# Batch 0 loads halved over two queues, filler matmuls on zeros, a revised start order, and one v cast moved to GpSimd, in a fused attention and channel-mix kernel

## The chip, the cores and the metric

The kernel runs on one core of one Trainium2 chip. The metric is the device time of one execution in microseconds; lower is better. The record marks each run as fast or slow (a program can fall into a slower state whatever its kernel). The kernel before took 221.51 us (median of 3 runs, 221.03 to 221.57). A profiled execution has a span a little shorter than its device time (219.7 us for a run of 221.48 us).

## The reference, cut to what matters

```python
# q, k, v: (batch 8, heads 8, seq 576, head_dim 64)
q_s = softmax(q, over head_dim)             # per row
k_s = softmax(k, over seq)                  # per column
kv  = einsum('bhsd,bhse->bhde', k_s, v)     # 64 x 64 per head
x   = einsum('bhsd,bhde->bhse', q_s, kv)    # -> (8, 576, 512)
x_prev = x shifted by one row
xk = mu_k * x + (1 - mu_k) * x_prev
xr = mu_r * x + (1 - mu_r) * x_prev
k  = relu(xk @ w_k)                         # 512 -> 1024
v  = (k * k) @ w_v                          # 1024 -> 512
out = sigmoid(xr @ w_r) * v
```

## The kernel before: the parts that matter

Two groups ("group 0" and "group 1") of four heads make up a batch. Each group goes through an attention pass: exp of q and of k and a cast of v (ScalarE), a softmax sum and scaling of q (VectorE), kv and transposes and x (TensorE), copies out of PSUM (ScalarE), then difference and mix into xk and xr (VectorE). The second half, the "units" of 512, 384 or 256 columns, multiplies xk by w_k (tile kfp), takes a relu on ScalarE (rel), squares on VectorE (k2), multiplies by w_r (rp) and w_v (vp).

The start is written out by hand; everything after it is ordered by a scheduler when the program is built.

```python
def emit_load(b, g, queues=None):
    t = ldpool.tile([128, 3, 2, J * D], F32, tag="raw", name="raw")
    for i, src in enumerate((q, k, v)):
        ...                                  # 576 KB each
        queue = queues[i] if queues else nc.gpsimd
        ld.append(queue.dma_start(out=t[:, i, :, :], in_=ap))

first = emit_load(0, 0, (nc.sync, nc.scalar, nc.sync))
...                                          # mu
emit_load(0, 1, (nc.scalar, nc.sync, nc.scalar))
...
emit_weights(first[2])                       # w_k, w_r, w_v on the GpSimd queue, after batch 0's first v
emit_load(1, 0)                              # batch 1, same queue, behind the weights
emit_load(1, 1)
with tc.manual_schedule(engines={PE, DVE, Activation}):   # shortened
    emit_mu()
    a0 = Attention(0, 0); a1 = Attention(0, 1)
    a0.exp(0); a0.exp(1); a0.norm_q(); a0.cast_v(nc.scalar.copy)
    a1.exp(0)
    a0.kv("mm"); a0.transpose_q(); a0.copy_qt(); a0.weights()
    a1.exp(1); a1.norm_q()
    a0.x(0); a0.x(1)
    a1.cast_v(nc.scalar.copy)
    a1.kv("mm"); a1.transpose_q(); a1.copy_qt()
    a0.diff(); a0.mix(0)
    a1.weights()
    a1.x(0); a1.x(1); a1.diff(); a1.mix(0)
    a0.mix(1); a1.mix(1)
...                                          # then units, with attention of later batches between their pieces
for pair in range(B // 2):
    for c0, n in UNITS:
        advance(...)
        for c in unit(pair, c0, n, 4 if pair == 0 and c0 == 0 else 1):
            cols += c
            advance(...)                     # so many attention steps of later batches
```

The softmax here doesn't subtract the row's maximum and nothing guards it: scores larger than these inputs give would overflow.

Of the kernel before, what the change touches and what calls it, by code (L numbers as in the profile page):

```python
# [13 lines left out]
BF16 = mybir.dt.bfloat16  # L14
# [4 lines left out]
def kernel(  # L19
# [18 lines left out]
    nc = tc.nc  # L38

    B, H, S, D = q.shape  # L40
# [3 lines left out]
    J = S // 64  # L44
# [5 lines left out]
    const = ctx.enter_context(tc.tile_pool(name="const", bufs=1))  # L50
# [10 lines left out]
    SYNC = mybir.DependencyInfo(mybir.DependencyClass.Sync, mybir.DependencyReason.DATA)  # L61
    ctx.enter_context(tc.manual_schedule(engines={mybir.EngineType.Pool}))

    def emit_load(b: int, g: int, queues=None):
        t = ldpool.tile([128, 3, 2, J * D], F32, tag="raw", name="raw")
        ld = []
        for i, src in enumerate((q, k, v)):
            ap = bass.AP(tensor=src.tensor,
                         offset=src.offset + (b * H + 2 * g) * S * D,
                         ap=[[J * D, 128], [4 * S * D, 2], [1, J * D]])  # L70
            queue = queues[i] if queues else nc.gpsimd
            ld.append(queue.dma_start(out=t[:, i, :, :], in_=ap))  # L72
        raw[b, g] = t
        return ld

    first = emit_load(0, 0, (nc.sync, nc.scalar, nc.sync))
    mu_sb = const.tile([8, 128], F32, name="mu_sb")
    for m, src in enumerate((moe_mu_k, moe_mu_r)):
        ap = bass.AP(tensor=src.tensor, offset=src.offset, ap=[[64, 4], [256, 2], [1, 64]])
        nc.sync.dma_start(out=mu_sb[4 * m:4 * m + 4, :].rearrange("p (u e) -> p u e", u=2),  # L80
                          in_=ap)
    emit_load(0, 1, (nc.scalar, nc.sync, nc.scalar))
    warm = const.tile([1, 1], F32, name="warm")
    nc.vector.memset(warm[:], 0.0)
    nc.scalar.activation(out=warm[:], in_=warm[:], func=ACT.Exp)


    ident = const.tile([128, 128], BF16, name="ident")
    make_identity(nc, ident[:])
    identf = const.tile([8, 8], F32, name="identf")  # L90
# [18 lines left out]
    def emit_weights(gate):  # L109
        def part(dst, src, n, u, c0, c1):  # L110
            ap = bass.AP(tensor=src.tensor, offset=src.offset + 4 * u * D * n + c0,
                         ap=[[n, 64], [D * n, CT], [1, c1 - c0]])
            return nc.gpsimd.dma_start(out=dst[64 * u:64 * u + 64, :, c0:c1], in_=ap)

        for h in range(2):
            for u in range(2):
                ld = part(wk_bf, moe_w_k, F, u, 512 * h, 512 * h + 512)
                if gate is not None:
                    tc.add_manual_dep(ld.ins, gate.ins.name, SYNC)
                gate = None  # L120
        for u in range(2):
            part(wr_bf, moe_w_r, C, u, 0, C)
        n = FT // 2
        for h in range(2):
            ap = bass.AP(tensor=moe_w_v.tensor,
                         offset=moe_w_v.offset + h * n * 128 * C,
                         ap=[[C, 128], [128 * C, n], [1, C]])
            nc.gpsimd.dma_start(out=wv_bf[:, h * n:(h + 1) * n, :], in_=ap)
# [3 lines left out]
    def emit_mu():  # L132
        mup = psum.tile([128, 8], F32, tag="mm", bufs=4, name="mup")
        nc.tensor.transpose(out=mup[:], in_=mu_sb[:], identity=identf[:])  # L134
        nc.vector.tensor_copy(out=mu[:], in_=mup[:])
# [2 lines left out]
    xpair = {}  # L138
    box = [0]

    class Attention:
        def __init__(self, b: int, g: int):
            self.b, self.g = b, g
            self.t = raw.pop((b, g))
            self.vv = vvs[box[0] % 3]
            self.xb = xbs[box[0] % 3]
            box[0] += 1
            if b // 2 not in xpair:
                xpair[b // 2] = (xpool.tile([128, CT, 2 * S], BF16, tag="xk", name="xk"),
                                 xpool.tile([128, CT, 2 * S], BF16, tag="xr", name="xr"))  # L150
            self.eqk = apool.tile([128, 2, J, 2, D], BF16, tag="eqk", name="eqk")
# [19 lines left out]
                out=self.qs[:].rearrange("p j (u d) -> p (j u) d", u=2), in0=eq,  # L171
                in1=rrec[:, :, None].to_broadcast((128, 2 * J, D)), op=ALU.mult)

        def kv(self, tag: str):
            if tag == "att":
                t = psum.tile([128, 2, 512], F32, tag="att", bufs=2, name="kvp")
                self.kvp = [t[:, 0, :], t[:, 1, :]]
            else:
                self.kvp = [psum.tile([128, 512], F32, tag="mm", bufs=4, name="kvp")[:, :]
                            for _ in range(2)]  # L180
            for j in range(J):
                for hf in range(2):
                    r = slice(64 * hf, 64 * hf + 64)
                    nc.tensor.matmul(  # L184
                        self.kvp[hf][:, 0:129],
                        lhsT=self.eqk[r, 1, j, :, :].rearrange("p u d -> p (u d)"),
                        rhs=self.vv[r, j, 0:129], start=(j == 0), stop=(j == J - 1))
# [18 lines left out]
            self.qt = apool.tile([128, J, 128], BF16, tag="qt", name="qt")  # L206
            nc.scalar.copy(out=self.qt[:], in_=self.qtp[:, 0:J, :])  # L207

        def x(self, hf: int):
            self.xp = psum.tile([128, 1024], F32, tag="att", bufs=2, name="xp")  # L210
            for c, e in ((0, 8), (8, J)):
                nc.tensor.matmul(self.xp[:, 64 * c:64 * e], lhsT=self.w[:, hf, :],  # L212
                                 rhs=self.qt[:, c:e, 64 * hf:64 * hf + 64],
                                 start=True, stop=True)
            nc.scalar.copy(out=self.xb[:, hf, 64:64 + S], in_=self.xp[:, 0:S])  # L215
# [90 lines left out]
            pass  # L306


    emit_weights(first[2])
    emit_load(1, 0)  # L310
    emit_load(1, 1)
    with tc.manual_schedule(engines={mybir.EngineType.PE, mybir.EngineType.DVE,
                                     mybir.EngineType.Activation}):
        emit_mu()
        a0 = Attention(0, 0)
        a1 = Attention(0, 1)
        a0.exp(0)
        a0.exp(1)
        a0.norm_q()
        a0.cast_v(nc.scalar.copy)  # L320
        a1.exp(0)
        a0.kv("mm")
        a0.transpose_q()
        a0.copy_qt()
        a0.weights()
        a1.exp(1)
        a1.norm_q()
        a0.x(0)
        a0.x(1)
        a1.cast_v(nc.scalar.copy)  # L330
        a1.kv("mm")
        a1.transpose_q()
        a1.copy_qt()
        a0.diff()
        a0.mix(0)
        a1.weights()
        a1.x(0)
        a1.x(1)
        a1.diff()
        a1.mix(0)  # L340
        a0.mix(1)
        a1.mix(1)
# [57 lines left out]
```

## Time and profile before

| kernel before | |
|---|---|
| device time | 221.51 us |
| TensorE busy, 60 to 200 us | 138.25 of 140 us |
| first exp of batch 1 (q, group 0) | 28.95 us, after a 3.68 us wait for its data |
| xk of group 1 ready | 27.8 us |
| first relu | 30.02 us |

First the activity rows of the profile page. Each digit is the busy share, in tenths, of one fortieth of the span (5.5 us here); PEclk is the TensorE clock that was granted, in tenths of full speed.

```profile
PE   0156599988999999999999999999999999999991
...
ACT  2645279999977779676929696949736392644340
...
PEclk9999969999999999999999999999999999999999
DMA  6999999999999791897085220232131400340414
```

TensorE has little to do in the first four or five slices and is full from then on. The DMA engines are full from 5 us on, for a dozen slices.

The same in stretches: start and end in us and length, then busy time of TensorE, of weight loads, of VectorE, ScalarE and GpSimd, the granted clock, the DMA share and the GB/s moved.

```profile
20.00:30.00 10.00, 7.08 (x27) 3.08 (x26) 5.46 (x15) 3.35 (x4) 4.26 (x6) 0.88 1.16 288
30.00:40.00 10.00, 9.78 (x67) 4.62 (x66) 9.36 (x20) 10.00 (x17) 3.74 (x6) 0.95 1.04 391
40.00:60.00 20.00, 18.34 (x141) 9.58 (x140) 19.93 (x45) 20.00 (x29) 8.31 (x12) 1.00 1.03 400
60.00:80.00 20.00, 19.92 (x140) 10.71 (x139) 19.79 (x46) 15.16 (x26) 4.95 (x7) 1.00 0.94 348
80.00:200.00 120.00, 118.33 (x810) 61.82 (x809) 96.54 (x223) 83.33 (x136) 6.35 (x9) 1.00 0.35 105
```

From 60 us on TensorE idles 1 to 2% of the time.

ScalarE's timeline around 24 us: start, duration, engine, line, operation, output and input, count, and in brackets the idle time before it and what ended that.

```profile
24.09 1.18 ACT L215 CAST xb_109<-xp 128x576 bf16<-128x576 f32 x2 [1.92 <-PE xp L212]
28.95 1.16 ACT L154 ACTIVATE eqk<-raw 128x1152 bf16<-128x1152 f32 x1 [3.68 <-DMA raw<-in_q_dram]
30.02 1.07 ACT L276 ACTIVATE rel<-kfp 128x512 bf16<-128x512 f32 x2
30.97 1.16 ACT L154 ACTIVATE eqk<-raw 128x1152 bf16<-128x1152 f32 x1
32.03 1.08 ACT L276 ACTIVATE rel<-kfp 128x512 bf16<-128x512 f32 x2
```

The first line is group 1's x, copied out of PSUM. Then ScalarE waits 3.68 us for batch 1's q, and from there exps and relus alternate.

TensorE's timeline, the same columns:

```profile
20.80 2.77 PE L270 MATMUL kfp<-xk,wk_bf 128*128 128x512 bf16 x6
23.36 1.10 PE L212 MATMUL xp<-qt,w 128*128 128x512 bf16 x4
24.30 0.59 PE L270 MATMUL kfp<-xk,wk_bf 128*128 128x512 bf16 x2
27.82 6.73 PE L270 MATMUL kfp<-xk,wk_bf 128*128 128x512 bf16 x23 [2.92 <-DVE xk L232]
...
35.84 1.03 PE L284 MATMUL rp<-wr_bf,xr 128*128 128x512 bf16 x4
```

Six kfp matmuls take 2.77 us, about 0.43 us from one to the next; in the second half of the 23 they come every 0.216 us. In the slow part the granted clock is 0.50 (28 to 31 us). (From 20 to 24 us the profile gives a clock of 1.00, although the matmuls there are just as slow. So early in a span the spacing of the matmuls is the safer sign, and the first digits of PEclk are not to be relied on.) The wait of 2.92 us is for group 1's xk.

VectorE makes that xk first and takes batch 1's softmax sum (rsum) afterwards:

```profile
27.01 0.76 DVE L232 TENSOR_TENSOR xk<-xm,xb_109 128x1152 bf16<-128x1152 bf16 x1
...
31.64 1.35 DVE L166 TENSOR_REDUCE rsum<-eqk 128x18 f32<-128x1152 bf16 x1
```

### The profile page before, as it was taken

What the parts mean: (1) busy time and instruction counts of PE and PEld (TensorE: products, weight loads), DVE (VectorE), ACT (ScalarE), POOL (GpSimd) and SP (SyncE); (2) the same over time, 40 slices, a digit from 0 to 9 for tenths busy, and PEclk for the clock granted to TensorE, in tenths of its full rate; (3) what the DMA queues carried; (4) which work ended last, traced back from release to release, by engine and by line L of the source; (5) the groups of instructions that cost most, each with busy time, mean ns of one, the idle gap of its engine ahead of it and who ended that gap; (6) DMA issues with size and microseconds to landing.
All of it is one profiled execution on the core that took longest, in us unless ns stands there. A gap on an engine that the chain in (4) does not pass through costs nothing.

```text
span 219.7 us, 3641 instructions
## 1 busy us (share of the span) xinstructions
PE 193.5 (88%) x1313; PEld 101.6 (46%) x1313; DVE 166.3 (76%) x384; ACT 147.7 (67%) x230; POOL 35.8 (16%) x56
## 2 busy tenths in 40 slices
PE   0156599988999999999999999999999999999991
PEld 0134134534547454445557443546465444554650
DVE  1196389999999998889798998888787758483431
ACT  2645279999977779676929696949736392644340
POOL 1294252433431210230030000000000000000000
PEclk9999969999999999999999999999999999999999
DMA  6999999999999791897085220232131400340414
GB/s 215 397 158 199 262 402 388 393 400 403 404 393 406 273 343 71 256 298 288 3 264 201 49 51 0 57 90 48 36 88 24 95 3 22 73 95 5 108 36 95
DMA packets 16171, 40.62 MB, mean 185 GB/s; under 512 B 2072, under 2 KB 4632, under 8 KB 16152
## 3 DMA queue, kind: packets, MB, share of 16 engines
q0 software_dynamic: 8736, 27.40, 38.0%
q1 hardware_dynamic: 6600, 11.22, 18.0%
q10 hardware_dynamic: 816, 1.77, 2.2%
q8 instruction: 10, 0.16, 0.3%
q14 instruction: 9, 0.07, 0.1%
HBM read 33.56 MB, written 9.44 MB: 196 GB/s over the span
## 4 chain that ended last, share of the span: by engine, by line
PE 60%; ACT 19%; DVE 13%; DMA 3%; issue 2%; SPq 1%; DVEq 0%; ACTq 0%
PE vp L291 22%; PE kfp L270 19%; PE rp L284 11%; ACT eqk L154 5%; ACT qt L207 4%; ACT rel L276 4%; DMA mu_sb<-in_moe_mu_r_dram 3%; PE kvp L184 3%; PE qtp L202 3%; PE xp L212 2%; DVE rsum L166 2%; DVE xk L232 2%; DVE qs L170 2%; ACT xb_105 L215 2%; ACT xb_109 L215 1%
## 5 line engine op out<-in xcount | busy, mean ns | idle before, releaser
L270 PE MATMUL kfp<-xk,wk_bf 128*128 128x384 bf16 (+2 forms) x384 | 72.6, 335 | 4.3 <-DVE xk L232 3.7
L276 ACT ACTIVATE rel<-kfp 128x512 bf16<-128x512 f32 (+2 forms) x96 | 45.4, 518 | 20.5 <-PE kfp L270 19.5
L270 PEld LDWEIGHTS <-wk_bf 128*128 128x128 bf16 x384 | 36.3, 99 | 30.3 <-issue 8.5
L154 ACT ACTIVATE eqk<-raw 128x1152 bf16<-128x1152 f32 x32 | 37.5, 1204 | 9.7 <-DMA raw<-in_q_dram 5.9
L294 DVE SCALAR_TENSOR_TENSOR ot<-th,vp 128x512 f32<-128x512 f32 x36 | 24.6, 683 | 17.3 <-PE vp L291 12.5
L287 ACT ACTIVATE th<-rp 128x512 f32<-128x512 f32 x36 | 22.7, 631 | 21.7 <-PE rp L284 20.7
L284 PE MATMUL rp<-wr_bf,xr 128*128 128x512 bf16 x144 | 37.0, 379 | 0.0
L207 ACT COPY qt<-qtp 128x1152 bf16<-128x1152 bf16 x16 | 18.2, 1136 | 7.7 <-PE qtp L202 7.5
L166 DVE TENSOR_REDUCE rsum<-eqk 128x18 f32<-128x1152 bf16 x16 | 21.6, 1348 | 1.6 <-ACT eqk L154 1.5
L170 DVE TENSOR_TENSOR qs<-eqk,rrec 128x1152 bf16<-128x1152 bf16 x16 | 21.7, 1355 | 0.8
L230 DVE TENSOR_SCALAR xm<-xd,mu 128x576 bf16<-128x576 bf16 x64 | 21.6, 378 | 0.4
L284 PEld LDWEIGHTS <-xr 128*128 128x128 bf16 x144 | 13.3, 98 | 13.8
L72 POOL DMA_DIRECT2D raw<-in_q_dram x14 | 10.0, 713 | 52.9 <-ACT vv_111 L160 24.0
L212 PE MATMUL xp<-qt,w 128*128 128x512 bf16 x64 | 13.5, 302 | 2.6 <-ACT qt L207 2.3
L184 PEld LDWEIGHTS <-eqk 64*128 64x128 bf16 x288 | 9.4, 100 | 9.2 <-issue 8.3
L202 PE MATMUL qtp<-ident,qs 128*128 128x128 bf16 x144 | 11.6, 231 | 1.5 <-DVE qs L170 1.5
L202 PEld LDWEIGHTS <-qs 128*128 128x128 bf16 x144 | 9.8, 103 | 4.1 <-DVE qs L170 1.8
L212 PEld LDWEIGHTS <-w 128*128 128x128 bf16 x64 | 6.3, 103 | 11.0 <-issue 6.1
L72 POOL DMA_DIRECT2D raw<-in_v_dram x14 | 10.0, 711 | 8.4 <-DMA raw<-in_q_dram 5.8
L72 POOL DMA_DIRECT2D raw<-in_k_dram x14 | 10.0, 711 | 5.7 <-DMA raw<-in_v_dram 3.0
L195 DVE SCALAR_TENSOR_TENSOR w<-kvp,rz,mask 128x128 bf16<-128x128 f32 x32 | 9.7, 345 | 0.0
L134 PE MATMUL mup<-identf,mu_sb 8*128 8x8 f32 x1 | 0.2, 243 | 9.8 <-DMA mu_sb<-in_moe_mu_r_dram 9.8
(83 smaller groups left out, 238.7 us busy)
## 6 DMA issues: line engine op xcount, KB each, us to landing
out_dram<-ot SPq DMA_DIRECT2D x72, 128.0 KB, 2.4
raw<-in_q_dram POOLq DMA_DIRECT2D x14, 576.0 KB, 12.4
raw<-in_k_dram POOLq DMA_DIRECT2D x14, 576.0 KB, 12.7
raw<-in_v_dram POOLq DMA_DIRECT2D x14, 576.0 KB, 13.1
wk_bf<-in_moe_w_k_dram POOLq DMA_DIRECT2D x4, 256.0 KB, 6.5
wv_bf<-in_moe_w_v_dram POOLq DMA_DIRECT2D x2, 512.0 KB, 12.4
raw<-in_k_dram ACTq DMA_DIRECT2D x1, 576.0 KB, 5.6
raw<-in_q_dram SPq DMA_DIRECT2D x1, 576.0 KB, 5.2
```

The source lines that it names most:

```text
L72: ld.append(queue.dma_start(out=t[:, i, :, :], in_=ap))
L154: nc.scalar.activation(out=self.eqk[:, i, :, :, :], in_=self.t[:, i, :, :].rearrange("p u (j d) -> p j u d", d=D), func=ACT.Exp)
L166: nc.vector.reduce_sum(out=rsum[:], in_=eq, axis=AX.X)
L170: nc.vector.tensor_tensor(out=self.qs[:].rearrange("p j (u d) -> p (j u) d", u=2), in0=eq, in1=rrec[:, :, None].to_broadcast((128, 2 * J, ...
L202: nc.tensor.transpose(out=self.qtp[:, j, :], in_=self.qs[:, j, :], identity=ident[:])
L207: nc.scalar.copy(out=self.qt[:], in_=self.qtp[:, 0:J, :])
L212: nc.tensor.matmul(self.xp[:, 64 * c:64 * e], lhsT=self.w[:, hf, :], rhs=self.qt[:, c:e, 64 * hf:64 * hf + 64], start=True, stop=True)
L270: nc.tensor.matmul(kfp[:, 0:n], lhsT=wk_bf[:, ct, fc * 128:(fc + 1) * 128], rhs=xk[:, ct, c0:c0 + n], start=(ct == 0), stop=(ct == CT - 1))
L276: nc.scalar.activation(out=rel[:, 0:n], in_=kfp[:, 0:n], func=ACT.Relu, scale=HALF_ROOT)
L284: nc.tensor.matmul(rp[:], lhsT=xr[:, ct, c0 + 128 * m:c0 + 128 * m + 128], rhs=wr_bf[:, ct, :], start=(ct == 0), stop=(ct == CT - 1))
L291: nc.tensor.matmul(vp[:], lhsT=k2[:, ft, 128 * m:128 * m + 128], rhs=wv_bf[:, ft, :], start=(ft == 0), stop=(ft == FT - 1))
L294: nc.vector.scalar_tensor_tensor(out=ot[:], in0=th[:], scalar=1.0, in1=vp[:], op0=ALU.add, op1=ALU.mult)
```

## The change

Its intent is to shorten the start. The two head blocks of each batch 0 load go as separate halves over the SyncE and the ScalarE queue, in the order in which they are needed. Matmuls on a tile of zeros fill TensorE's idle time, so that the slow clock is left earlier. mu moves off the front of TensorE and VectorE. Group 1's v cast goes to GpSimd, which takes 1.2 us off ScalarE; batch 1's loads, issued by GpSimd too, come after that cast.

```diff
-            queue = queues[i] if queues else nc.gpsimd
-            ld.append(queue.dma_start(out=t[:, i, :, :], in_=ap))
+            if b > 0:
+                ld.append(nc.gpsimd.dma_start(...))
+            else:
+                for u, queue in ((0, nc.sync), (1, nc.scalar)):
+                    ld.append(queue.dma_start(out=t[:, i, u, :], ...))
...
+    zeros = const.tile([128, 512], BF16, name="zeros")
+    nc.vector.memset(zeros[:], 0.0)
...
+    def filler(dst, count: int):
+        for _ in range(count):
+            nc.tensor.matmul(dst, lhsT=zeros[:, 0:128], rhs=zeros[:], start=True, stop=True)
...
-    emit_weights(first[2])
-    emit_load(1, 0)
-    emit_load(1, 1)
+    emit_weights(first[5])
     with tc.manual_schedule(...):
-        emit_mu()
         a0 = Attention(0, 0)
         a1 = Attention(0, 1)
         a0.exp(0)
+        a0.norm_q()
         a0.exp(1)
-        a0.norm_q()
         a0.cast_v(nc.scalar.copy)
+        a0.kv("mm", 20)              # 20 filler matmuls first
+        a0.transpose_q()
+        a0.weights()
         a1.exp(0)
-        a0.kv("mm")
-        a0.transpose_q()
         a0.copy_qt()
-        a0.weights()
+        a1.cast_v(nc.gpsimd.tensor_copy)
+        emit_load(1, 0)
+        emit_load(1, 1)
         a1.exp(1)
         a1.norm_q()
-        a0.x(0)
+        a0.x(0, 5)
         a0.x(1)
-        a1.cast_v(nc.scalar.copy)
-        a1.kv("mm")
+        emit_mu()
+        a1.kv("mm", 4)
         a1.transpose_q()
         a1.copy_qt()
+        a1.weights()
         a0.diff()
         a0.mix(0)
-        a1.weights()
-        a1.x(0)
+        a1.x(0, 4)
         a1.x(1)
```

## The prediction

> **What bounds the kernel now.** Three stretches, from the windows and the timeline. (a) 0 to 27.8 us: TensorE mostly waits, at last 2.9 us for VectorE's xk of group 1, ready at 27.8 (waits view). (b) 36 to 58 us: the chain of waits is nearly all ScalarE (20.0 of 20 us busy in 40:60; TensorE 18.3). (c) After 58 us TensorE is busy 97 to 100%. DMA is full from 5 to 70 us, 393 GB/s on raw inputs. Batch 1's first q, queued behind 5.2 MB of weights, lands only at 28.9 us; ScalarE waits 3.7 us for it.
>
> **What the change offers.** Smaller first pieces, mu off the front of TensorE and VectorE, one cast (1.17 us) off ScalarE, filler against the slow clock. In the trace 512-column matmuls come every 0.427 us until about 31 us (granted clock 0.50 at 28 to 31) and every 0.216 us after; the first long row has about 8 slow ones, 1.8 us. The Trainium skill, "TensorE: Matmul & The Clock Gate", Part 1, says that a busy window releases the clock and an idle one (3.4 us) takes it away; the trace agrees with the first half. As meant, xk of group 1 could be ready near 22 us: minus 5 or 6 us.
>
> **What the built order does.**
> 1. ScalarE's queue holds six load issues, the last two waiting for earlier loads to land (semaphore reuse), all ahead of the activation table load (1.28 us). First exp: about 8 us instead of 5.97. Hidden by 2.
> 2. ScalarE now has exp of batch 1's q BEFORE the two copies of group 1's x, and exp k, the v cast and both exps of batch 1's group 1 BEFORE the first relu. Before, the x copies ran at 24.1 us and relus were interleaved. VectorE has batch 1's sum and scaling ahead of group 1's mix; TensorE has kv of batch 1 ahead of the second half of kfp. All wait for batch 1's data. Splitting loads doesn't bring those earlier: bytes are the same, DMA was already full ("DMA: Bandwidth & Descriptors", Issuing engines are not separate DMA queues: all interleave on the same 16 engines; the trace shows no more than about 400 GB/s with three queues).
>
> **Sum from trace durations.** q lands 28.9; exp to 30.0; x copies to 31.1; VectorE sum, shift, reciprocal, diff, scale, mix, add (1.35+0.2+0.27+0.77+1.36+0.65+0.77) to about 35.5: xk of group 1 comes 7.7 us later than 27.8. TensorE idles from about 21 to 33 and is slow again. The first unit's kfp, with batch 1's kv, transposes, x and first rp, ends near 44.2 instead of 37.5 (+6.7 on TensorE); ScalarE in the same state near 44.8 against 40.6 (+4.2). TensorE's idle time between 36 and 58 (about 1.8 us) absorbs some: net about +5.
>
> **Prediction: 226.3 us**, range 223.0 to 230.0. Chances: faster 0.07, same 0.38, slower 0.55.
>
> **What would show it.** Right: exp of batch 1's q ends a ScalarE wait of some 8 us at about 29, group 1's x copies follow it; kfp waits for xk until about 35; TensorE nearly idle 21 to 33, clock down afterwards; first relu about 36; from 60 us on the same picture, some 5 us later. First exp near 8 us.
> Wrong: batch 1's q landing under 20 us, or kfp complete by 30.
>
> **What would make it wrong.** A changed later order winning back more of the delay; batch 1 landing earlier; GpSimd's cast so slow that batch 1's loads, queued behind it, come late (worse).

## The result, and the profile after

The changed kernel took 227.63 us (median of 4 runs, 227.11 to 228.13), against 221.3 us for the kernel before on the same chip: a ratio of 1.0286 (95% interval 1.025 to 1.0321). It is slower. Ratios in this document are the mean time of one kernel's fast runs over that of the other's of the same rounds, so they are not quite the ratio of the medians quoted beside them. The results were correct here and in all experiments.

The activity rows, each slice 5.6 us:

```profile
PE   7595029999699999999999999999999999999991
...
ACT  0971098999982969694966969677928293544340
...
PEclk9999656999999999999999999999999999999999
DMA  6999999999999338299239040232042310440414
```

TensorE is now busy in the first four slices, with filler and a faster start, and then nearly empty in the fifth and sixth. ScalarE is nearly empty in the fourth and fifth. The clock is lost right after and shows low values in three slices.

```profile
20.00:30.00 10.00, 1.25 (x6) 0.39 (x4) 0.81 (x1) 2.00 (x3) 2.95 (x5) 0.68 1.14 314
30.00:40.00 10.00, 7.62 (x47) 4.12 (x48) 9.97 (x23) 8.51 (x11) 4.26 (x6) 0.63 1.03 392
40.00:60.00 20.00, 17.26 (x126) 8.70 (x125) 19.06 (x38) 19.92 (x26) 8.48 (x12) 1.00 1.03 397
60.00:80.00 20.00, 19.89 (x139) 11.25 (x138) 18.85 (x47) 14.98 (x30) 2.12 (x3) 1.00 0.77 279
80.00:200.00 120.00, 118.33 (x819) 61.43 (x818) 98.24 (x227) 82.39 (x132) 8.47 (x12) 1.00 0.37 110
```

These are the stretches in the order of the table before. From 20 to 40 us TensorE is busy 8.87 us, where before it was busy 16.86 us. From 60 us on the two kernels are alike: the loss is all in the beginning.

ScalarE's timeline shows why:

```profile
28.00 1.16 ACT L167 ACTIVATE eqk<-raw 128x1152 bf16<-128x1152 f32 x1 [10.14 <-DMA raw<-in_q_dram]
29.07 1.16 ACT L230 CAST xb_117<-xp 128x576 bf16<-128x576 f32 x2
30.12 1.17 ACT L167 ACTIVATE eqk<-raw 128x1152 bf16<-128x1152 f32 x1
31.18 1.15 ACT L173 CAST vv_119<-raw 128x1152 bf16<-128x1152 f32 x1
32.59 1.16 ACT L167 ACTIVATE eqk<-raw 128x1152 bf16<-128x1152 f32 x1 [0.26 <-DMA raw<-in_q_dram]
34.02 1.16 ACT L167 ACTIVATE eqk<-raw 128x1152 bf16<-128x1152 f32 x1 [0.26 <-DMA raw<-in_k_dram]
35.48 0.60 ACT L291 ACTIVATE rel<-kfp 128x512 bf16<-128x512 f32 x1 [0.30 <-PE kfp L285]
```

Batch 1's exp now stands ahead of the two copies of group 1's x. It waits 10.14 us for its data, and the copies wait behind it, though their input was there at 18.56 us (the xp matmuls start at 17.91 us and take 0.65 us). Three more exps and a cast follow before the first relu. The long wait ends at 28 us in this kernel and at 28.95 us in the one before: splitting the loads of batch 0 did not bring batch 1 much earlier. What changed is what stands behind the wait.

VectorE, where batch 1's softmax sum and scaling stand before group 1's xk:

```profile
29.19 1.35 DVE L179 TENSOR_REDUCE rsum<-eqk 128x18 f32<-128x1152 bf16 x1 [9.88 <-ACT eqk L167]
...
31.52 1.35 DVE L183 TENSOR_TENSOR qs<-eqk,rrec 128x1152 bf16<-128x1152 bf16 x1
...
33.62 0.76 DVE L247 TENSOR_TENSOR xk<-xm,xb_117 128x1152 bf16<-128x1152 bf16 x1
```

And TensorE:

```profile
19.36 1.89 PE L285 MATMUL kfp<-xk,wk_bf 128*128 128x512 bf16 x8 [0.81 <-DVE xk L247]
32.38 1.16 PE L198 MATMUL kvp<-vv_119,eqk 64*128 64x129 bf16 x18 [11.13 <-ACT vv_119 L173]
...
34.43 3.30 PE L285 MATMUL kfp<-xk,wk_bf 128*128 128x512 bf16 x8
...
41.57 1.03 PE L299 MATMUL rp<-wr_bf,xr 128*128 128x512 bf16 x4
```

The first eight kfp matmuls come at the fast rate now, as the filler meant. Then TensorE is idle for 11.13 us, in front of batch 1's kv. Its clock is 0.50 afterwards, and the next eight kfp matmuls take 3.30 us: the fast clock that the filler won was lost before it was of use.

Group 1's xk is ready at 34.4 us instead of 27.8 us (+6.6), the first rp starts at 41.57 us instead of 35.84 us (+5.7), the first rp of the second unit at 63.96 us instead of 58.66 us (+5.3), the last rp at 217.84 us instead of 212.37 us (+5.5).

### The profile page after: what moved, and what is told of

Its sections match the earlier page's. It is cut to its first block, busy times and chain, and to the rows that moved or that the text cites. A ratio compares the mean times of both kernels' runs of the same rounds, so it can differ in the third digit from the quotient of the medians.

```text
span 225.3 us, 3726 instructions
## 1 busy us (share of the span) xinstructions
PE 199.7 (89%) x1346; PEld 104.0 (46%) x1346; DVE 167.2 (74%) x385; ACT 147.7 (66%) x229; POOL 36.9 (16%) x57
## 4 chain that ended last, share of the span: by engine, by line
PE 64%; DVE 11%; ACT 10%; DMA 9%; POOL 3%; issue 1%; ACTq 0%; DVEq 0%
PE vp L306 25%; PE kfp L285 18%; PE rp L299 12%; DMA raw<-in_q_dram 6%; PE kvp L198 3%; PE xp L227 3%; ACT eqk L167 3%; DMA raw<-in_v_dram 3%; ACT qt L221 2%; ACT rel L291 2%; PE qtp L216 2%; DVE xk L247 2%; DVE rsum L179 2%; DVE xm L245 2%; POOL wk_bf L121 1%
## 5 line engine op out<-in xcount | busy, mean ns | idle before, releaser
L285 PE MATMUL kfp<-xk,wk_bf 128*128 128x384 bf16 (+2 forms) x384 | 70.8, 330 | 3.4 <-DVE xk L247 2.8
L302 ACT ACTIVATE th<-rp 128x512 f32<-128x512 f32 x36 | 22.1, 613 | 23.0 <-PE rp L299 21.9
L227 PE MATMUL xp<-qt,w 128*128 128x512 bf16 x64 | 12.9, 285 | 1.7 <-ACT qt L221 1.2
L198 PE MATMUL kvp<-vv_119,eqk 64*128 64x129 bf16 x90 | 4.0, 236 | 11.1 <-ACT vv_119 L173 11.1
```

The costliest lines, as they stand in the source:

```text
L227: nc.tensor.matmul(self.xp[:, 64 * c:64 * e], lhsT=self.w[:, hf, :], rhs=self.qt[:, c:e, 64 * hf:64 * hf + 64], start=True, stop=True)
L285: nc.tensor.matmul(kfp[:, 0:n], lhsT=wk_bf[:, ct, fc * 128:(fc + 1) * 128], rhs=xk[:, ct, c0:c0 + n], start=(ct == 0), stop=(ct == CT - 1))
```

## The experiments

The theory: the cost is the ORDER of instructions on ScalarE (and after it on VectorE and TensorE). Work of batch 1, whose data cannot be there before 28 us, stands ahead of work of batch 0. The rivals: the filler matmuls cost time or clock; six load issues ahead of ScalarE's first exp cost time; the split loads are slower; the cast is slower on GpSimd.

The order can be seen without running, in the built program. Building variants of the diff, only one word of it was found to decide the order on ScalarE: with `a1.cast_v(nc.scalar.copy)` in the otherwise unmodified changed kernel, group 1's x copies stand before batch 1's exp again, with the relus in between as in the kernel before. Leaving out the filler, or the split loads, does not restore it (e2 and e3 show this). e9 and e10 run both sides of this.

| run | what it is | median us | ratio to before (95%) |
|---|---|---|---|
| e1 | before, one exp put ahead | 228.78 | 1.0316 (1.0288 to 1.0344) |
| e2 | changed, no filler | 226.91 | 1.0240 (1.0203 to 1.0278) |
| e3 | changed, whole loads | 229.13 | 1.0338 (1.0307 to 1.0369) |
| e4 | changed, order put right | 219.87 | 0.9914 (0.9885 to 0.9944) |
| e5 | before, with e4's order | 225.73 | 1.0162 (1.0098 to 1.0226) |
| e6 | e4, no filler | 220.11 | 0.9933 (0.9877 to 0.9988) |
| e7 | e4, whole loads | 221.05 | 0.9977 (0.9950 to 1.0003) |
| e8 | e4, cast on ScalarE | 219.50 | 0.9907 (0.9843 to 0.9972) |
| e9 | changed, cast on ScalarE | 222.22 | 1.0042 (1.0015 to 1.0068) |
| e10 | before, cast on GpSimd | 228.61 | 1.0337 (1.0315 to 1.0359) |
| e11 | e4, one more edge on VectorE | 219.09 | 0.9906 (0.9877 to 0.9934) |
| e12 | changed, w_v loaded last | 220.57 | 0.9985 (0.9937 to 1.0033) |

e1 to e4, e5 to e8 and e9 to e11 shared a chip and the runs of before within each set; e12 had its own. The kernel before took 221.24 to 221.81 us in them. Where kernels of different sets are compared below (e4 with e6, e7, e8 and e11 above all), the chips differ, and only the ratios to before are a fair measure.

### e1_before_exp_ahead: the order alone, put into the kernel before

```diff
         a1.weights()
+        early[1, 0] = Attention(1, 0)
+        early[1, 0].exp(0)
         a1.x(0)
```

(The attention pass of batch 1 then takes this object instead of making its own.)

> The kernel before, with one instruction moved: batch 1's first exp (q, group 0) stands on ScalarE ahead of the two copies of group 1's x. No filler, no split loads, nothing on GpSimd. Order theory: the exp waits for its data until about 28.9 us, the x copies end about 31.1 instead of 25.3, xk of group 1 is ready about 33.6 instead of 27.8, and the kernel takes 225 to 227 us (4 to 5.5 us over before). Rivals (filler, six issues on ScalarE, split loads, GpSimd cast are the cost): nothing of theirs is in this kernel, so 221.3, the same as before, within 0.7 us.

Measured: 228.78 us, 1.0316.

```profile
28.60 1.16 ACT L154 ACTIVATE eqk<-raw 128x1152 bf16<-128x1152 f32 x1 [6.47 <-DMA raw<-in_q_dram]
29.67 1.16 ACT L215 CAST xb<-xp 128x576 bf16<-128x576 f32 x2
```

The exp waits until 28.60 us, the x copies follow, group 1's xk is ready at 34.7 us. The order alone costs as much as the whole change, with none of its other parts present, so no rival is needed for a loss of this size. (That the rivals are not the cause in the changed kernel itself is shown by e4, which keeps them all and has no loss, and by e9.) It cost more than I expected: VectorE followed, with batch 1's softmax sum ahead of the mix, so xk came 1.1 us later than I had added up. ScalarE also has three exps and a cast ahead of the first relu, but that relu (35.84 us) waited 1.46 us more for its kfp, so xk was the later of the two.

### e2_after_no_filler and e3_after_whole_loads: two parts undone, the order left

```diff
 def filler(dst, count):            # e2
-    for _ in range(count):
+    for _ in range(0):
```

e3 restores `emit_load` and the queues of the kernel before.

> The changed kernel without the 33 filler matmuls, all else and ScalarE's order as built. Order theory: everything waits for batch 1's q at about 28, so filler neither costs nor gains: 227.0 to 228.2. Rival (filler is the cost, by its own time or by the clock that is granted): 221 to 224.

> The changed kernel with the six whole batch 0 loads of the kernel before (three issues on ScalarE instead of six). ScalarE's order after the start as in the changed kernel. Order theory: the first exp comes near 6 us instead of 7.5, yet the time stays 226.8 to 228.2, since batch 1's q lands at 28 to 29 either way. Rival (splitting and the six issues are the cost): 221 to 224.

Measured: 226.91 us (226.46 to 228.03) and 229.13 us (228.91 to 229.46). Both stay slow, so neither part is the cost. e2 lies just below what I expected (227.0 to 228.2); its interval overlaps that of the changed kernel, so whether filler costs a few tenths here is not settled. e3 has its first exp at 6.16 us instead of 7.53 us, and that gained nothing. It missed my range on the upper side. In its profile batch 1's q was late, 29.46 us against 28.00 us.

This landing orders all five profiled runs that have the inverted order, roughly: exp of batch 1's q started at 28.00 (changed), 28.60 (e1), 28.70 (e2), 28.92 (e10) and 29.46 us (e3), and these executions took 227.11, 228.57, 228.03, 228.56 and 228.91 us. It fits a start that is gated by that one landing. Why the landing moves by a microsecond from run to run was not found out.

### e4_after_ordered: the change with the order put right

```diff
+NOSYNC = ...                       # an ordering edge between instructions of one engine, no wait
 # every exp and v cast of batch 1:
+if self.b == 1:
+    tc.add_manual_dep(e.ins, held["rel"].ins.name, NOSYNC)   # after the first unit's eighth relu
 # pacing: no attention step is emitted between the first unit's relus
     cols += c
+    if cols <= 512 * FT:
+        continue
     advance(...)
```

> The changed kernel with the order alone put right: ordering edges without waits hold ScalarE's exps and casts of batch 1 behind the eight relus of the first unit, and the pacing puts no attention step between those relus. Order theory: group 1's x copies at about 18.4 us, xk of group 1 about 21.7, all eight relus done by about 28, TensorE in the fast clock there; the time falls below BEFORE: 214 to 219 us. Rivals: filler, split loads, GpSimd cast are all still in it: 226 to 228.

Measured: 219.87 us, 0.9914, 7.8 us less than the changed kernel's median (1.0286). The loss is gone and a gain of 0.9% is there. It is less than I expected (214 to 219 us). The start does what was meant, as ScalarE's timeline shows:

```profile
19.65 1.18 ACT L236 CAST xb<-xp 128x576 bf16<-128x576 f32 x2 [0.49 <-PE xp L233]
24.01 2.26 ACT L297 ACTIVATE rel<-kfp 128x512 bf16<-128x512 f32 x4 [3.18 <-PE kfp L291]
27.47 2.06 ACT L297 ACTIVATE rel<-kfp 128x512 bf16<-128x512 f32 x4 [1.20 <-PE kfp L291]
29.39 1.19 ACT L169 ACTIVATE eqk<-raw 128x1152 bf16<-128x1152 f32 x1
```

The eight relus fill the time in which batch 1 is awaited. But the lead is given back. Starts of milestones, in us, read from TensorE's timelines (the profiled execution of each):

| | before | changed | e4 | e9 | e11 |
|---|---|---|---|---|---|
| first rp | 35.84 | 41.57 | 28.56 | 36.85 | 30.06 |
| first rp of the second unit | 58.66 | 63.96 | 55.05 | 58.93 | 53.23 |
| tenth rp group | 85.92 | 91.39 | 84.14 | 86.16 | 83.57 |
| last rp but one | 209.78 | 215.25 | 208.03 | 210.02 | 207.09 |

e4 is 7.3 us ahead at the first rp, 3.6 us at the second unit, 1.8 us from 84 us to the end. In between VectorE is full:

```profile
60.00:80.00 20.00, 18.85 (x145) 10.60 (x145) 20.00 (x47) 15.01 (x25) 4.24 (x6) 1.00 0.99 368
```

(e4's stretch from 60 to 80 us: TensorE 18.85, VectorE 20.00 of 20 us.) So TensorE arrives early and waits for VectorE: just before 50 us it waits 1.29 us for a scaled q (qs) and 0.85 us for xk. A second loss shows in the second unit's kfp matmuls, here in e4 and then in e11:

```profile
49.77 5.45 PE L291 MATMUL kfp<-xk,wk_bf 128*128 128x384 bf16 x24 [0.85 <-DVE xk L253]
49.32 4.07 PE L293 MATMUL kfp<-xk,wk_bf 128*128 128x384 bf16 x24 [1.61 <-DVE xk L255]
```

In e4's profiled execution the granted clock is 0.50 from 50 to 52 us and 0.69 from 52 to 53; in e11's it is 1.00. The same 24 matmuls take 1.4 us longer in e4, a good third of the 3.7 us of lead lost by the second unit.

### e5_before_ordered: e4's order alone, on the kernel before

The edges and the pacing of e4, on the unmodified kernel before.

> The kernel before, unchanged in its start, with the pacing and the ordering edges of e4 alone (eight relus of the first unit ahead of batch 1's exps). It asks whether e4's gain of 0.9% is the order by itself. If order by itself gains: 218 to 220. My theory: it does not, because in this start xk of group 1 is ready only at 27.8, so the relus end near 35 and batch 1's exps, which before filled ScalarE from 29 on, now wait for them: ScalarE loses about 2 to 3 us, 222.5 to 225.5.

Measured: 225.73 us (222.94 to 226.0), 1.0162, which the record calls unclear, and just above what I expected (222.5 to 225.5). With the old start the relus are not through until about 35.6 us, and batch 1's exp, which could have run at 28.95 us, starts at 35.62 us. The first rp is even 1.0 us earlier than before (34.80 us), but the second unit's is 2.5 us later (61.19 us). So e4's order is not good by itself. It pays only with a start that is done before batch 1 lands, and then the change's faster start is worth 5 to 6 us (225.73 to 219.87, on two chips).

### e6_ordered_no_filler, e7_ordered_whole_loads, e8_ordered_cast_scalar: what each part is worth in the right order

The edits of e2 and e3 on e4, and for e8:

```diff
-        a1.cast_v(nc.gpsimd.tensor_copy)
+        a1.cast_v(nc.scalar.copy)
```

> e4 without the 33 filler matmuls. If filler does what it is meant for: the first 8 kfp matmuls and more run at 0.427 us each, the eight relus end 1 to 2 us later, and the time rises by up to that, 220.5 to 222. My theory: most of it is hidden by batch 1's landing, 219.6 to 221.0, whatever the granted clock shows.

> e4 with the six whole batch 0 loads. In e3 batch 1's q landed 1.46 us later than in the changed kernel (29.46 against 28.00) and the time was 1.5 us longer. If that landing is what follows the loads: again about 1 to 1.5 us later and 220.5 to 221.8. If whole loads are as good: 219.5 to 220.2.

> e4 with the second v cast back on ScalarE. The cast takes 1.05 us of ScalarE at about 14 us; if that delays the second half of the start it is xk of group 1 about 1 us later and 220.2 to 221.2; if the wait for v of group 1 set the time anyway: 219.5 to 220.2. Batch 1's loads no longer stand behind the cast in GpSimd's queue: no effect expected, as the DMA is full.

Measured: 220.11 us (218.62 to 221.26), 221.05 us (219.74 to 221.16) and 219.50 us (218.02 to 220.80). All three lie in ranges that I had named. The runs of these kernels scatter by 1.4 to 2.8 us, and the intervals of e6 and e8 overlap e4's. Filler does its work locally: without it the first eight kfp matmuls take 3.10 us, with it 1.89 us. The first rp of the profiled run comes at 29.96 us instead of 28.56 us in e4, but e8 and e11, which have the filler, had theirs at 29.68 and 30.06 us, so that difference is not shown to be the filler's. In the total the means differ by 0.2%, within noise. The interval of e7 lies just above e4's (from 0.9950, where e4's ends at 0.9944), so whole loads may cost 0.6%; as the two ran on different chips, this is not settled. The cast's engine makes no difference once the order is held by edges: 0.9907 against 0.9914. On the trace the cast takes 1.24 us on GpSimd and 1.13 to 1.17 us on ScalarE in the start; the Trainium skill, "GPSIMD Engine Reference", 4.1 Engine selection, calls an operation with one input "roughly line-rate" on GpSimd, in a comparison with VectorE. No such cast ran on VectorE here; against ScalarE the trace shows a difference of about 0.1 us.

### e9_after_cast_back: one word undone

The one-line edit of e8, on the changed kernel, without ordering edges.

> The changed kernel with ONE word undone: the second v cast runs on ScalarE again, as before. Built, it shows that this alone puts group 1's x copies back ahead of batch 1's exps, with two relus after each of them, as in the kernel before; split loads, filler and the revised order are all still in it. Theory (the cast's engine decides the order, the order costs the time): exp of batch 1's q at 28 to 29 after the x copies, first relu right after it at about 29.2, xk of group 1 by 24; the loss is gone and the time is 218.5 to 221.5. Rivals (filler, split loads or the six issues cost 6 us): 226 to 228.

Measured: 222.22 us (221.64 to 222.72), 1.0042: 5.4 of the 6.3 us of loss are gone with this one word, and filler, split loads and six issues are all still in. I had expected 218.5 to 221.5 us, so this is a miss on the upper side. ScalarE's timeline and then TensorE's show what stayed:

```profile
20.34 1.18 ACT L230 CAST xb<-xp 128x576 bf16<-128x576 f32 x2 [0.49 <-PE xp L227]
28.88 1.16 ACT L167 ACTIVATE eqk<-raw 128x1152 bf16<-128x1152 f32 x1 [7.36 <-DMA raw<-in_q_dram]
29.95 1.06 ACT L291 ACTIVATE rel<-kfp 128x512 bf16<-128x512 f32 x2
```

```profile
24.46 1.89 PE L285 MATMUL kfp<-xk,wk_bf 128*128 128x512 bf16 x8 [1.22 <-DVE xk L247]
30.58 4.98 PE L285 MATMUL kfp<-xk,wk_bf 128*128 128x512 bf16 x15 [4.23 <-ACT rel L291]
```

The x copies are early (20.34 us) and xk is early, sixteen kfp matmuls are done by 26.4 us. Then TensorE waits 4.23 us for a relu to free PSUM, and the relu waits behind batch 1's exp until 28.88 us. So here too the wait for batch 1 gates the first unit, and the faster start is worth nothing: the first relu comes at 29.95 us, and at 30.02 us in the kernel before. This is why the change could not have gained in that kernel's order either.

### e10_before_cast_gpsimd: that word alone, on the kernel before

```diff
-    emit_load(1, 0)
-    emit_load(1, 1)
...
-        a1.cast_v(nc.scalar.copy)
+        a1.cast_v(nc.gpsimd.tensor_copy)
+        emit_load(1, 0)
+        emit_load(1, 1)
```

> The kernel before with only that part of the change done: the second v cast on GpSimd, and batch 1's loads issued after it (as in the changed kernel; otherwise the cast would stand behind six load issues). No filler, whole loads, old order. Built, it has the same inverted order as the changed kernel. Theory: exp of batch 1's q waits until about 28.8 with the x copies behind it, xk of group 1 about 34.7, as in e1; 227.5 to 229.5. Rivals: an offloaded cast of 1.2 us is no loss: 220.5 to 222.

Measured: 228.61 us (228.41 to 229.29), 1.0337, inside the expected range.

```profile
28.92 1.16 ACT L154 ACTIVATE eqk<-raw 128x1152 bf16<-128x1152 f32 x1 [8.95 <-DMA raw<-in_q_dram]
29.99 1.16 ACT L215 CAST xb<-xp 128x576 bf16<-128x576 f32 x2
```

The same inversion, the same loss. Moving a cast of 1.2 us off ScalarE cost 7 us, through the order in which the scheduler then put other instructions.

### e11_ordered_vector_too: one more edge

```diff
-            nc.vector.reduce_sum(out=rsum[:], in_=eq, axis=AX.X)
+            rs = nc.vector.reduce_sum(out=rsum[:], in_=eq, axis=AX.X)
+            if self.b == 2:
+                tc.add_manual_dep(rs.ins, held["mix", 1, 1].ins.name, NOSYNC)
```

> e4 and one more ordering edge, on VectorE: batch 2's softmax sum (and with it its scaling, together 2.9 us) stands behind the mix that completes batch 1's xk. In e4, 7.3 us ahead of before at the first rp, all but 3.6 us was gone at the second unit's first rp, and VectorE had batch 2's sum and scaling ahead of that xk (ready 49.7). If that is where the gain went: xk about 47, second unit's first rp about 52.5 instead of 55, and 217 to 219. If VectorE's amount of work to 80 us is the limit (20.0 of 20 us busy from 60 to 80 in e4), the delay comes back later and the time stays 219 to 220.5.

Measured: 219.09 us, 0.9906: not to be told from e4. The edge moved batch 2's sum behind the mix, as meant (the mix at 48.52 us, the sum at 50.27 us), but xk came at 49.3 us, not at the 47 us that I expected, against 49.7 us in e4. The second unit's first rp came at 53.23 us instead of 55.05 us, though this execution's first rp was 1.5 us later. Of these 1.8 us, 1.4 are the slow clock of e4's execution (the two kfp lines above) and only 0.4 an earlier xk; whether the edge kept the clock is not shown. Then the lead shrank again, with VectorE busy 20.00 of 20 us from 60 to 80. It fits that VectorE's amount of work up to 80 us takes back what an earlier start gains; it was not tested by taking VectorE work away, and remains an argument.

### e12_after_wv_last: batch 1 ahead of w_v

```diff
         emit_load(1, 0)
         emit_load(1, 1)
+        emit_wv()                  # the two w_v loads, before this ahead of batch 1
```

> The changed kernel with one thing moved: the two loads of w_v (2 MB) are issued after batch 1's six loads instead of ahead of them, cast still on GpSimd. Two effects are meant. Batch 1's q should land about 5 us earlier (2 MB at about 400 GB/s), near 23 us; and built, the order changes too: group 1's x copies stand before batch 1's exps, but exp q, exp k and the v cast of batch 1's group 0 still stand before the first relu. Theory (ScalarE's wait for batch 1's landing gates the first unit in every order seen so far): first exp of batch 1 at 22.5 to 24, first relu at 26 to 27.5, w_v landing near 35 to 36 and TensorE waiting some 2 to 4 us for it before the first vp; 217 to 221. If batch 1's landing does not gate: the time stays within 1 us of e9, 221.5 to 223; if the late w_v costs as much as the early q gains: the same.

Measured: 220.57 us (220.03 to 223.30, five runs), 0.9985. Batch 1's q was there at 22.60 us, 5.4 us earlier, as expected from the bytes, and the first relu came at 26.91 us. The late w_v cost no wait, where I had expected 2 to 4 us: the first vp followed the first rp without a gap, at 35.88 us. The first rp, 35.02 us, was 6.6 us earlier than in the changed kernel. The order changed in the same build (x copies before batch 1's exps), so this run does not separate the landing from the order. VectorE kept the bad order: the x copies ended at 19.45 us, but batch 1's sum, which waited for the exp, stood ahead of group 1's xk, and TensorE waited 4.69 us for that xk, until 25.86 us. It shows that the loss can be removed at the loads too, with the cast left on GpSimd. A sixth run, of 224.99 us, is slow and is left out; a fast one took 223.30 us, which was not looked into.

## Why the prediction was right, point by point

- "Batch 1's q lands only at 28.9 us", whatever is done to batch 0's loads: right. The wait ended at 28.00 us in the profiled run. The Trainium skill, "DMA: Bandwidth & Descriptors", Issuing engines are not separate DMA queues, says that transfers from all issuing engines end up on the same 16 DMA engines and interleave; the traces agree as far as they go: 391 to 400 GB/s in both kernels from 30 to 60 us, and the same landing within a microsecond. What moved the landing was fewer bytes ahead of it (22.60 us in e12).
- "ScalarE now has exp of batch 1's q BEFORE the two copies of group 1's x" and the relus after four exps and casts: right, and shown to be the cause by e1 (order alone, +3.2%), e9 (order nearly undone by one word, +0.4%) and e10 (that word alone, +3.4%).
- "First exp: about 8 us instead of 5.97. Hidden by 2": right. It was 7.53 us, and e3, with the first exp at 6.16 us, was no faster.
- "TensorE idles from about 21 to 33 and is slow again": right. It was idle 11.13 us up to 32.38 us. The granted clock fell to 0.50 within the idle stretch (0.84 from 23 to 24 us, 0.50 from 24 us on), about 2.4 us after the last kfp matmul; the Trainium skill, "TensorE: Matmul & The Clock Gate", Part 1, puts the idle window at about 3.4 us and calls it free-running. Only the order of size agrees: 2.4 us here, and 2.8 us in the kernel before (last matmul done at 24.9 us, clock 0.84 from 27 to 28 us), were enough, so a whole idle window is not needed in these traces.
- The sum: +5 predicted, +6.3 us measured between the medians (5.6 us between the spans). The delay was smaller than I said and the recovery much smaller. Group 1's xk came 6.6 us late, not 7.7; the first rp 5.7 us late, not 6.7, and the landing, 0.9 us earlier than assumed, accounts for most of either difference. But of these 5.7 us only 0.4 were absorbed up to 58.7 us, where I had counted on some 1.8 us ("TensorE's idle time between 36 and 58 absorbs some"). That term of the sum is the mis-sized one: ScalarE was busy 19.92 of 20 us from 40 to 60 and TensorE waited there in this kernel as well (17.26 of 20 us, 18.34 before). A delay put too high and a recovery put too high partly cancel, so the mechanism was right, but that the sum came so near is in part luck. Also, two of the four runs took 227.1 us and two 228.1 us; the profile is of a 227.1 us one, and the other microsecond is not explained.
- What the prediction did not see is that the single word of the cast made the order. It took the built order as a fact, which was enough for the number.
- "As meant, xk of group 1 could be ready near 22 us: minus 5 or 6 us": half right. e4 has that xk at 23.3 us and is 7.3 us ahead at the first rp, but the total is only 0.9% better than before, since the lead is given back between 29 and 84 us.

Left open: why the scheduler orders ScalarE differently when a cast moves to GpSimd; how much of the loss is due to ScalarE's order and how much to VectorE's and TensorE's, which changed with it; the run-to-run movement of batch 1's landing; whether VectorE's load or the slow clock near 50 us is what limits e4, and what limits e11; and whether filler is worth anything in the total.

## What to carry to other kernels

In these traces ScalarE worked through its queue in order: two copies that were ready at 18.56 us stood behind an exp that waited for a load until 28.00 us, and ran only at 29.07 us. So look for any instruction that waits for a load with ready work behind it. After any edit, even one that only moves an operation to another engine, compare the order of the instructions on every engine, and look for work of the next batch standing ahead of work of this one. A faster start is worth only what the next gate lets through: find the landing, or the full engine, that will hold it, before you count the gain.

## What the Trainium skill lacked or had wrong

- No page says that a tile scheduler may reorder other instructions when one operation changes its engine, or that the built order should be compared: one word cost 3.4% (e10). It belongs to "Perfetto Trace Analysis", Identifying Dependency Chains.
- "TensorE: Matmul & The Clock Gate" says that operands of all zeros do not trip the current limit; it does not say whether matmuls on zeros release the slow clock. They do: of 20 back to back from 1.23 us, the first 13 came about every 0.427 us, the rest, from about 6.7 us, every 0.216 us.
- The same page has no rule for a window in which TensorE was busy for a part: the clock fell about 2.4 us (changed kernel) and 2.8 us (before) after the last matmul.
- "ScalarE: Activation LUTs", What ACT_TABLE_LOAD costs, gives 1.28 us for the load and another 1.38 us for a drain at every switch to a different set. The load took 1.28 us here too, but the next instruction followed at once (load at 6.13 us, next at 7.42 us): after the first load of a program no such drain shows. One before the load would be hidden in the wait that ends at 6.13 us, and no run here switches sets.
- "DMA: Bandwidth & Descriptors" advises against splitting a transfer into two partition halves and against spreading loads over queues for bandwidth. It says nothing of a split by heads, so that work can start on the first half. Here that brought nothing forward (group 0's v cast at 9.66 us in e4, at 9.46 us with whole loads in e7), though split loads may make the whole 0.6% better (e4 against e7, intervals just apart, on two chips).
